# One-token attention and MLP on one core: row-form MLP products, a compact residual, w1 and w2 loaded behind the query weights, whole last K/V blocks

## The chip, the cores and the metric

The kernel runs on one core of a Trainium2 chip. The metric is device time in microseconds (us), from the start to the end of one execution; the number for a kernel is the median of its runs. The engines are PE (matrix products), DVE (vector), ACT (scalar), POOL (GpSimd) and SP, which here only issues transfers. Each engine runs its own instructions in order and waits on semaphores. SBUF is on-chip memory with 128 partitions, PSUM holds the results of PE in eight banks, and 16 DMA engines move data from HBM.

## The reference

```python
xn = _layernorm(x)
# attention: 32 query heads, 4 K/V heads, 65536 keys of 128, bf16
q = xn @ wq
p = softmax(q @ k^T * 128**-0.5); o = p @ v
A = o.reshape(1, 1, 4096) @ wo
# MLP branch on xn, S = 1
h  = gelu(layernorm(xn) @ w1)          # 1024 -> 1024
hs = concatenate([g0, g1, g2, g3]) @ w2
x1 = xn + hs
B  = x1 + gelu(layernorm(x1) @ w3) @ w4   # 1024 -> 3584 -> 1024
return x + A + B
```

g0 to g3 are the four quarters of h shifted along the sequence; with a sequence of one token each of them is zero, so the kernel multiplies w2 with a zero vector `g_bf`. K and V together are 134.2 MB; wq and wo are 8.4 MB each, w1 and w2 2.1 each, w3 and w4 7.3 each. The output is 1024 numbers in bf16.

## The kernel before

**Queues.** The kernel is written as five lists of operations (`_Q`), one an engine, in program order. `_op` and `_grp` append an operation or a group to a list and put the needed semaphore waits ahead of it, worked out from objects `_B` that remember the last write and the reads of a buffer. All large loads are issued by SP, in the order of the program, into one hardware queue.

**Attention.** The keys of a K/V head are cut into 8 tiles of 8192 keys, 32 tiles in all (`NT`). K and V come in blocks of two tiles, 4.19 MB each, 16 blocks of either (`issue_k(m)`, `issue_v(m)`, line 279), into two slots of `Kn` and `Vn`. Only the last block of K and of V (m = 15) is loaded as two halves (line 288), so that tile 30 needs only the first. I call these blocks K0 to K15 and V0 to V15. For tile n:
- `Ttr` (line 470): four DVE transposes of 128x1024 bring a tile of K into `X`;
- `QK` (480): 16 products of 512 columns into `S_ps`, on four column groups of PE at once;
- `stats1`, `MB`, `stats2`: the maximum over a row on DVE, spread over the partitions by a small product;
- `EXP` (508): the exponential on ACT; `PTr`: a product that orders the probabilities, and a DVE transpose `pT_f`;
- `PV` (531): 16 products with `Vn` into `OT_ps`; `FLASH` (541): ACT copies the result, POOL scales and adds it into `O_acc`.

The transposes of tile n+1 stand among tile n's DVE work: the first of them directly ahead of tile n's maximum (`Ttr(n + 1, [0])`, then `stats1(n)`), the others behind `EXP` and `PTr`. At the end of tile n the request for K block n/2+2 (even n) or V block (n-1)/2+2 (odd n) goes to SP's list; it waits until the slot is free, that is, until both tiles of the old block are transposed (K) or multiplied (V).

**Combine.** After the 8 tiles of a head, `combine_1` (553) sums and inverts the denominators and builds `cb_W`; `combine_2` (561) forms the head's normalized output with four f32 products (line 564) and three small DVE steps, giving `o_bf`. The combine of heads 0 to 2 stands inside the first tile of the next head; that of head 3 at the end.

**Weights.** The query weights are loaded first into slot 1 of `Kn` and `Vn`. A 14336-column buffer `W` holds w1, then w2, the halves of w3, wo of heads 0 and 1 in turn: each is loaded after one tile (0, 4, 8, 12, 16, 20) and multiplied after another (3, 7, 11, 15, 19, 23). w1, w2 and w3 are multiplied in column form (`mm_cols`, 362): the weight is the stationary operand, 128x128 at a time, and one column streams, so the result lies along the partitions. `out_resid` (409) adds the residual `acc` to the output with 32 small f32 products against an identity.

**Output.** `OUT_ps` collects 1024 outputs as rows of 256 on four partitions. `out_rows` (400, products at line 404) multiplies a stationary column of `o_bf` or `gh_bf` with rows of wo or w4, four products of 256 columns a row. Each group waits for the group before it, since all write `OUT_ps`.

**The end.** After tile 29 wo of heads 2 and 3 is requested; after tile 30, when K's slots are free, w4 in parts of 14, 8, 4 and 2 rows. PE's order behind tile 31 is: wo of head 2, combine of head 3, wo of head 3, w4 part by part. Then DVE casts the 4x256 outputs (line 631) and SP stores them.

## Time and profile before

| | |
|---|---|
| median of 3 runs | 402.89 us (402.86 to 402.99) |
| profiled execution, its span | 401.7 us; no time of its own is given for it beside the span, the median lies 1.2 us above |
| busy: DVE, PE, POOL, ACT | 228.4, 186.4, 61.8, 48.9 us |
| read from HBM | 169.87 MB, 423 GB/s over the span |
| mean granted PE clock | 0.586 |
| DVE waits for K | 67.4 us in 11 waits, the longest 9.2 |

The profile is one execution. Its first part gives the busy time of each engine; a second one cuts the span into 40 slices of 10 us, one digit a slice (9 is 90% busy or more), with the clock that PE was granted and the traffic. The table of DMA queues gives packets, megabytes and the share of the 16 engines' time. In the timeline a line has the start, the busy time, the engine, the line of the kernel, the operation, what it writes and reads, and in brackets the idle time before it and what ended that. Weight loads of PE (PEld) run beside the products.

### The profile page before, as it was taken

The page shows a single profiled execution, that of the slowest core. Times are in us where ns is not written, and L with a number is a line of the kernel's source. Part 1 is how long each engine was busy: PE and PEld are TensorE (multiplying, and loading weights), DVE is VectorE, ACT ScalarE, POOL GpSimd, SP SyncE. Part 2 cuts the span into 40 slices and gives each one's busy share as a digit, 9 for nine tenths or more (in the row PEclk, how much of TensorE's full clock was granted, in tenths as well). Part 3 has the DMA queues.
Part 4 walks back from the last instruction along what each step waited for, and adds up shares of the span by engine and source line. Part 5 has one row for each costly group of instructions (what it writes and reads, how often), then busy time and mean ns, then how long its engine had stood idle before and what let it go on. Part 6 is the DMA issues. An engine that isn't in the chain of part 4 may idle for free.

```text
span 401.7 us, 4776 instructions
## 1 busy us (share of the span) xinstructions
PE 186.4 (46%) x1859; PEld 78.5 (20%) x1875; DVE 228.4 (57%) x401; ACT 48.9 (12%) x128; POOL 61.8 (15%) x90
## 2 busy tenths in 40 slices
PE   0332325064525745285531965353433654444664
PEld 0211101021103511062110731121111311111132
DVE  0247566277816578255744287576836775788410
ACT  1000111011101011011110011111201111112100
POOL 5000003012211011110310101111110112112110
PEclk9985556556565556555655555656555656565566
DMA  8999999999999999999999999999999999999994
GB/s 359 424 418 438 445 418 424 460 419 421 436 447 419 429 435 435 422 436 445 420 428 450 426 419 441 441 419 428 434 439 421 447 432 424 426 425 436 437 416 207
DMA packets 7087, 170.19 MB, mean 424 GB/s; under 512 B 916, under 2 KB 920, under 8 KB 1048
## 3 DMA queue, kind: packets, MB, share of 16 engines
q1 hardware_dynamic: 6920, 169.87, 98.4%
q8 instruction: 15, 0.25, 0.2%
q14 instruction: 8, 0.07, 0.0%
q10 hardware_dynamic: 144, 0.00, 0.0%
HBM read 169.87 MB, written 0.00 MB: 423 GB/s over the span
## 4 chain that ended last, share of the span: by engine, by line
DMA 55%; DVE 24%; PE 16%; issue 2%; ACT 1%; SPq 0%; another core or an unknown queue 0%; POOL 0%; ACTq 0%
DMA Kn<-in_A_k_cache_dram 44%; DVE X L476 13%; DMA Kn<-in_B_w_dram 6%; DMA Vn<-in_A_wq_dram 5%; PE H_ps L366 4%; PE S_ps L488 3%; DVE pT_f L529 3%; PE OT_ps L536 3%; DVE mrow L495 3%; PE M_ps L366 1%; ACT p_sb L518 1%; PE PT_ps L527 1%; PE M_ps L564 1%; PE OUT_ps L404 1%; DVE Yall L393 1%
## 5 line engine op out<-in xcount | busy, mean ns | idle before, releaser
L476 DVE STREAM_TRANSPOSE X<-Kn 128x1024 f32<-128x1024 f32 x128 | 151.7, 1215 | 67.4 <-DMA Kn<-in_A_k_cache_dram 67.4
L536 PE MATMUL OT_ps<-Vn,pT_f 128*32 128x512 bf16 x512 | 60.7, 627 | 52.4 <-DVE pT_f L529 52.4
L488 PE MATMUL S_ps<-X,Yall 128*32 128x512 bf16 x512 | 59.1, 608 | 16.1 <-DVE X L476 16.1
L501 PE MATMUL MB_ps<-Rm,Lmat 128*128 128x16 bf16 x32 | 6.1, 192 | 90.1 <-DVE Rm L496 90.1
L550 POOL TENSOR_TENSOR O_acc<-O_acc,tmpO 128x513 f32<-128x513 f32 x28 | 32.8, 1172 | 88.6 <-ACT tmpO L544 88.6
L518 ACT ACTIVATE p_sb<-S_ps,brun 128x512 bf16<-128x512 f32 x32 | 22.0, 687 | 192.7 <-DVE brun L516 157.3
L548 POOL TENSOR_SCALAR O_acc<-O_acc,ff 128x513 f32<-128x513 f32 x28 | 19.5, 698 | 153.4 <-ACT ff L523 153.4
L495 DVE TENSOR_REDUCE mrow<-S_ps 128x1 f32<-128x512 f32 x32 | 21.6, 674 | 25.5 <-PE S_ps L488 25.5
L544 ACT ACTIVATE tmpO<-OT_ps 128x512 f32<-128x512 f32 x32 | 19.1, 598 | 108.0 <-PE OT_ps L536 108.0
L488 PEld LDWEIGHTS S_ps<-X,Yall 128*32 128x32 bf16 x512 | 16.6, 126 | 54.7 <-DVE X L476 38.2
L529 DVE STREAM_TRANSPOSE pT_f<-PT_ps 128x512 f32<-128x512 f32 x32 | 22.9, 716 | 6.1 <-PE PT_ps L527 4.2
L536 PEld LDWEIGHTS OT_ps<-Vn,pT_f 128*32 128x32 bf16 x512 | 14.6, 129 | 59.2 <-DVE pT_f L529 42.0
L501 PEld LDWEIGHTS MB_ps<-Rm,Lmat 128*128 128x128 bf16 x32 | 3.3, 102 | 114.9 <-DVE Rm L496 114.9
L527 PE MATMUL PT_ps<-p_sb,permR 128*128 128x512 bf16 x16 | 9.3, 580 | 21.4 <-ACT p_sb L518 21.4
L366 PEld LDWEIGHTS H_ps<-xn_bf,W 128*128 128x128 bf16 x224 | 14.4, 169 | 1.7 <-issue 1.7
L366 PE MATMUL H_ps<-xn_bf,W 128*128 128x1 bf16 x224 | 14.5, 202 | 0.0
L527 PEld LDWEIGHTS PT_ps<-p_sb,permR 128*128 128x128 bf16 x32 | 3.4, 105 | 41.4 <-ACT p_sb L518 41.4
L505 DVE TENSOR_REDUCE Bst<-MB_ps 128x1 f32<-128x16 f32 x32 | 5.6, 174 | 8.3 <-PE MB_ps L501 8.3
L330 PE MATMUL M_ps<-ln_s,ones_f 128*128 128x1 f32 x6 | 1.8, 362 | 17.3 <-DVE ln_s L329 17.3
L546 POOL COPY O_acc<-tmpO 128x513 f32<-128x513 f32 x4 | 2.4, 612 | 47.4 <-ACT tmpO L544 47.4
L404 PE MATMUL OUT_ps<-Kn,gh_bf 128*1 128x256 bf16 x112 | 5.6, 364 | 5.0 <-DMA Kn<-in_B_w_dram 5.0
L631 DVE CAST orow<-OUT_ps 128x256 bf16<-128x256 f32 x1 | 0.4, 425 | 12.7 <-PE OUT_ps L404 12.7
(109 smaller groups left out, 116.6 us busy)
## 6 DMA issues: line engine op xcount, KB each, us to landing
Kn<-in_A_k_cache_dram SPq DMA_DIRECT2D x15, 4096.0 KB, 27.3
Vn<-in_A_v_cache_dram SPq DMA_DIRECT2D x15, 4096.0 KB, 23.3
W<-in_B_w_dram SPq DMA_DIRECT2D x2, 3584.0 KB, 24.9
W<-in_A_wo_dram SPq DMA_DIRECT2D x3, 2048.0 KB, 23.8
Kn<-in_A_wq_dram SPq DMA_DIRECT2D x1, 4096.0 KB, 12.1
Vn<-in_A_wq_dram SPq DMA_DIRECT2D x1, 4096.0 KB, 21.2
W<-in_B_w_dram SPq DMA_DIRECT2D x2, 2048.0 KB, 33.8
Kn<-in_A_k_cache_dram SPq DMA_DIRECT2D x2, 2048.0 KB, 25.3
```

Source lines behind the costliest of these rows:

```text
L366: fns.append(lambda e, j=j, cx=cx: e.matmul(ps_tile[:, c0 + cx:c0 + cx + 1], lhs_fn(j - j0, cx), rhs_fn(j), start=(j == 0 and cx == 0), st ...
L404: fns.append(lambda e, lhs=lhs, rhs=rhs, jj=jj: e.matmul(OUT_ps[32 * jj:32 * jj + 1, 0:256], lhs, rhs[:, 256 * jj:256 * jj + 256], start=F ...
L476: _op(q_dve, lambda e, ix=ix: e.transpose(out=X32[:, xs, 1024 * ix:1024 * (ix + 1)], in_=Kn32[:, s, 4096 * half + 1024 * ix:4096 * half + ...
L488: fns.append(lambda e, we=we, cm=cm, mv=mv: e.matmul(S_ps[32 * cm:32 * cm + 32, :], Yall[:, h, we, :, :].rearrange("p a g -> p (a g)"), mv ...
L495: _op(q_dve, lambda e: e.reduce_max(mrow[:, m:m + 1], S_ps[:, :], axis=AX.X), reads=[b_S], writes=[b_mrow[m]])
L518: _op(q_act, lambda e: e.activation(p_sb[:, m, :], S_ps[:, :], ACTF.Exp, bias=brun[:, kn:kn + 1], scale=SCALE, accum_out=tmpO[:, m, 512:513]),
L527: _op(q_pe, lambda e: e.matmul(PT_ps[:, :], permR[:, :], p_sb[:, m, :], start=True, stop=True), reads=[b_p[m], b_const], writes=[b_PT])
L529: _op(q_dve, lambda e: e.transpose(out=pT_f[:, :], in_=PT_ps[:, :]), reads=[b_PT], writes=[b_pT])
L536: fns.append(lambda e, q=q, q4=q4: e.matmul(OT_ps[32 * q4:32 * q4 + 32, :], pT_bf[:, q, :, 1], Vn[:, s, 8192 * half + 512 * q:8192 * half ...
L544: _op(q_act, lambda e: e.activation(tmpO[:, m, 0:512], OT_ps[:, :], ACTF.Copy), reads=[b_OT], writes=[b_tmpO[m]], partial=True)
L548: _op(q_pool, lambda e: e.tensor_scalar(out=O_acc[:, :], in0=O_acc[:, :], scalar1=ff[:, m:m + 1], scalar2=0.0, op0=ALU.mult, op1=ALU.add), ...
L550: _op(q_pool, lambda e: e.tensor_tensor(out=O_acc[:, :], in0=O_acc[:, :], in1=tmpO[:, m, :], op=ALU.add), reads=[b_tmpO[m]], writes=[b_Oacc])
```

## The change

1. `mm_rows` takes the place of `mm_cols` for w1, w2 and w3: now the vector is the stationary operand, spread over 32 columns, and the weights stream, 256 or 448 columns at a time on four column groups. The result lies in rows; `to_cols` turns it into columns (ACT copy out of PSUM, an f32 product with a selecting matrix, a masked DVE multiplication, a DVE sum). New constants for it: `selQ`, `selS`, `mask32`.
2. `out_resid` builds a masked 128x256 tile on DVE and needs four f32 products.
3. w1 and w2 are requested directly behind the query weights, ahead of K0 and V0, w2 into slot 1 of `X`; their whole chain (`w12_pe`) runs before tile 0, the first half of w3 is requested behind V1 and multiplied after tile 7, the second half requested after tile 8 and multiplied after tile 15; wo of head 0 requested after tile 16 and multiplied after tile 23.
4. The last K and V blocks are loaded whole.
5. `O_acc` is double; the combines of heads 0 and 1 move to the ends of tiles 15 and 23, that of head 2 to the end of the kernel. `cb_W` now lies in `pT_f`.
6. wo of head 3 is requested after tile 24, w4's first 16 rows after tile 28, wo of heads 1 and 2 after tile 29 into slot 0 of `Vn`, w4's other 6, 4 and 2 rows after tile 30. The order on PE behind tile 31 is in the diff.
7. Some operations count on semaphores of their own, and waits of an engine on its own semaphore are left out where a reader's wait covers them.

The diff, cut to its core:

```diff
@@ _deps
         for s, v in b.w.items():
-            q.wait((s, v))
+            if s is not q.sem or not b.r:
+                q.wait((s, v))
@@ start
         load_rows(Vn[:, 1, :], b_V[1], "wqb", A_wq, 4, 4)
+        load_rows(W[:, 0:8192], [b_W], "w", B_w1, 0, 8)
+        load_rows(X[:, 1, :], b_X[1], "w2", B_w2, 0, 8)
@@ issue_kv
-            if m < NPAIR - 1:
-                _dma(q_sp, chan("%s%d" % (ch, s)), lambda e: e.dma_start(out=t[:, s, :], in_=src), writes=b_t[s])
-            else:
-                for hf in range(2):
-                    _dma(q_sp, chan("%sh%d" % (ch, hf)), lambda e, hf=hf: e.dma_start(out=t[:, s, 8192 * hf:8192 * hf + 8192], in_=src[:, 8192 * hf:8192 * hf + 8192]),
-                         writes=[b_t[s][hf]])
+            _dma(q_sp, chan("%s%d" % (ch, s)), lambda e: e.dma_start(out=t[:, s, :], in_=src), writes=b_t[s])
@@ MLP
+        def mm_rows(outs, lhs_fn, rhs_fn, j0, nj, njt, reads):
             fns = []
+            for j in range(j0, j0 + nj):
+                for sg, (tile, jj, c0, ln, _) in enumerate(outs):
+                    fns.append(lambda e, j=j, sg=sg, tile=tile, jj=jj, c0=c0, ln=ln: e.matmul(
+                        tile[32 * jj:32 * jj + 32, c0:c0 + ln], lhs_fn(j).broadcast_to([P, 32]), rhs_fn(j, sg),
+                        start=(j == 0), stop=(j == njt - 1), tile_position=(0, 32 * jj), skip_group_check=True))
...
+        def to_cols(parts, ln, n_in, mask, dst, b_dst, more):
...
+            for a, (tile, c0, bt, _, _) in enumerate(parts):
+                _op(q_act, lambda e, a=a, tile=tile, c0=c0: e.activation(hsb[:, a, :], tile[:, c0:c0 + ln], ACTF.Copy),
+                    reads=[bt], writes=[b_Wt] + more, partial=(a > 0))
+            _grp(q_pe, [lambda e, a=a, sl=sl, p0=p0: e.matmul(M0_ps[p0:p0 + sl.shape[1], 0:ln], sl, hsb[:, a, :], start=True, stop=True)
+                        for a, (_, _, _, sl, p0) in enumerate(parts)], reads=[b_Wt, b_const], writes=[b_M0])
...
@@ out_resid
+            _grp(q_pe, [lambda e, jj=jj: e.matmul(OUT_ps[32 * jj:32 * jj + 1, 0:256], maskA[:, jj, 0:1], A4, start=True, stop=False,
+                                                  tile_position=(0, 32 * jj), skip_group_check=True) for jj in range(4)],
+                 reads=[b_Wt, b_const], writes=[b_OUT], partial=True)
@@ loop and end
-        w4_parts = [(0, 14, 0, 0), (14, 8, 1, 0), (22, 4, 1, 8), (26, 2, 0, 14)]
+        w4_parts = [(0, 16, 0, 0), (16, 6, 1, 0), (22, 4, 1, 6), (26, 2, 1, 10)]
+        w12_pe()
+        w3_dma(0)
         Ttr(0, range(4))
         for n in range(NT):
...
-            if nb == 0 and h > 0:
-                combine_1(h - 1)
...
-            if nb == 0 and h > 0:
-                combine_2(h - 1)
...
+            if n == 7:
+                w3_pe(0)
+            elif n == 15:
+                combine_1(0)
+                w3_pe(1)
+                combine_2(0)
+            elif n == 23:
+                combine_1(1)
+                wo_pe(0)
+                combine_2(1)
...
+            if n == NT - 4:
+                w4_free(0)
+            elif n == NT - 3:
+                wo_dma(1)
+                wo_dma(2)
+            elif n == NT - 2:
+                for i in range(1, len(w4_parts)):
+                    w4_free(i)
-        wo_pe(HKV - 2)
-        combine_1(HKV - 1)
-        combine_2(HKV - 1)
-        wo_pe(HKV - 1)
-        for i in range(len(w4_parts)):
+        combine_1(2)
+        combine_2(2)
+        combine_1(3)
+        w4_pe(0)
+        combine_2(3)
+        wo_pe(3)
+        wo_pe(1)
+        wo_pe(2)
+        for i in range(1, len(w4_parts)):
             w4_pe(i)
```

## The prediction

> **What bounds the kernel now.** I read the page first: the slices, then the table of DMA queues.

> ```profile
> span 401.7 us, 4776 instructions
> ...
> DMA  8999999999999999999999999999999999999994
> ...
> q1 hardware_dynamic: 6920, 169.87, 98.4%
> q8 instruction: 15, 0.25, 0.2%
> ```

> One queue moves 169.87 MB and keeps the 16 DMA engines 98.4% busy. No compute engine is above 57%. Only the first and last slices are below 9. So the time is start, plus bytes over rate, plus what follows the last byte; a compute edit costs nothing until the queue runs dry or the work after the last loads overruns them. Next I read the timeline of DVE and PE around the last K blocks.

> ```profile
> 342.57 1.25 DVE L476 STREAM_TRANSPOSE X<-Kn 128x1024 f32<-128x1024 f32 x1 [4.64 <-DMA Kn<-in_A_k_cache_dram]
> ...
> 355.59 3.46 DVE L476 STREAM_TRANSPOSE X<-Kn 128x1024 f32<-128x1024 f32 x3
> ```

> The first line is block K14 landing (tile 28). The three transposes of the second line are the last two of tile 29 and, without a pause, the first of tile 30: the first half of K15 was there. K12 ended the same wait at 303.72, so four blocks (V12, K13, V13, K14) of 4.19 MB take 38.85 us: 9.71 us a block, 432 GB/s. Last I read the timeline of the end.

> ```profile
> 379.73 1.90 PE L536 MATMUL OT_ps<-Vn,pT_f 128*32 128x512 bf16 x16 [0.81 <-DVE pT_f L529]
> ...
> 381.41 1.73 PE L404 MATMUL OUT_ps<-Vn,o_bf 128*1 128x256 bf16 x32
> ...
> 383.50 0.38 PE L554 MATMUL M_ps<-O_acc,Dmat_f 128*128 128x1 f32 x2 [0.36 <-POOL O_acc L550]
> ...
> 384.67 1.16 PE L564 MATMUL M_ps<-O_acc,cb_W 128*128 128x128 f32 x8 [0.78 <-DVE cb_W L557]
> ...
> 386.92 1.88 PE L404 MATMUL OUT_ps<-W,o_bf 128*1 128x256 bf16 x32 [1.09 <-DVE o_bf L571]
> 390.37 2.98 PE L404 MATMUL OUT_ps<-Kn,gh_bf 128*1 128x256 bf16 x56 [1.58 <-DMA Kn<-in_B_w_dram]
> 395.21 1.04 PE L404 MATMUL OUT_ps<-Kn,gh_bf 128*1 128x256 bf16 x32 [1.85 <-DMA Kn<-in_B_w_dram]
> 397.63 1.02 PE L404 MATMUL OUT_ps<-Kn,gh_bf 128*1 128x256 bf16 x16 [1.38 <-DMA Kn<-in_B_w_dram]
> 398.85 0.59 PE L404 MATMUL OUT_ps<-Kn,gh_bf 128*1 128x256 bf16 x8 [0.19 <-DMA Kn<-in_B_w_dram]
> ```

> The last PV product ends at 381.63, and from 390.37 on PE waits for w4. PE finished wo at 388.80, 1.57 us early: that is the whole reserve in front of w4. After the last load only 0.59 us of PE, 0.42 of DVE and the store remain. The fourth view is the busy time in stretches of 3.41 us, the step in which the granted clock changes (the last columns are the clock, DMA share and GB/s).

> ```profile
> 379.40:382.81 3.41, 3.08 (x44) 1.52 (x48) 0.27 (x1) 0.60 (x1) 0.45 (x1) 0.50 1.01 428
> 382.81:386.22 3.41, 1.87 (x22) 1.28 (x14) 0.98 (x4) 0.00 (x0) 0.64 (x1) 1.00 1.02 434
> 386.22:389.64 3.42, 1.88 (x32) 0.97 (x32) 0.52 (x2) 0.00 (x0) 0.00 (x0) 0.50 0.94 402
> ```

> Full clock comes for one stretch behind a stretch with PE busy 3.08 of 3.41, and goes again. So 32 output-row products cost 1.88 us at half clock (386.92) and 1.04 at full (395.21).

> **The change part by part.** The sum is made against the profiled span of 401.7 us, in which the last product ends at 399.44; the median of 402.89 is 1.2 us above it, and I add differences to the median.

> *Loads.* The bytes are the same. The two last blocks lose two issues on SP (0.33 to 0.43 us each), hidden while more than one block is queued. Fewer PE instructions: w1, w2 and w3 go from 64, 64 and 224 one-column products to 32, 32 and 64 rows, the residual from 64 records to 8, and three row-to-column steps add about 8. That is 272 of 1859 products, and as many weight loads. If the 15 instruction packets shrink in proportion, two go. By the queue table one holds a DMA engine 0.2% x 16 x 401.7 / 15 = 0.86 us. The slowest engine gains between 0 and 1.7; I take 0.3, near nothing, because each packet falls on one engine of 16.

> *Start.* w1 and w2 (4.19 MB) now go in front of K0 and V0, which land 9.7 us later. The whole w1/w2 chain runs before tile 0. It begins when the second layer norm ends, 33.4: two row products of 32 (1.88 each), two ACT copies (at most 0.60), two f32 products over 256 columns (half of 2.07, the four of line 564 at 138.84), two pairs of DVE passes over 256 columns (0.42 each, as the output cast), the gelu (six steps, 1.3), two adds (0.4), the residual (0.43 DVE, 1.03 PE) and a layer norm (29.77 to 33.37: 3.6). Sum 15.6, so the first transpose moves from 33.3 to 49.0. Queued behind it on DVE are all of tile 0's transposes, and behind those the request for K2 on SP, which moves from 46.17 to about 62. But the queue then holds V0, K1, V1 and the first half of w3, until about 80: the query weights land at 22.5 (the chain's first load, 1.25 + 21.25), w1 and w2 at 32.2, then four blocks at 9.71 and 3.67 MB of w3 (8.5). Cover 18 us; cost 0. The two new constants on POOL (0.2 + 0.4 each at 0.93 to 5.06) are made before x lands at 13.05; cost 0.

> *Middle.* The w3 step at tile 15 was 7.2 us of PE and 1.4 of gelu. Now it is about 3.3 for a half of w3 (32 products of 448 columns at 0.104), then two copies (1.2), two f32 products over 448 columns (3.6), two DVE passes (1.4) and the gelu, with the first head's combine among them. DVE waits for K 67.4 us in 11 waits, up to 9.2 long, and a K request lands 27.3 us after issue against 9.7 of transfer: 17 us of cover. Cost 0. Fewer semaphore waits inside a tile: DVE's gaps there are 0.03 us; between 0 and 0.2 over the last two tiles, I take 0.1. SP's order at the end is new: w4's 16 rows after tile 28, two wo loads after tile 29, the rest of w4 once tile 31 is transposed, near 377; K15, V15, w4's 16 rows and the two wo loads fill the queue until 391. Cover 14; cost 0.

> *Last blocks whole.* K15 lands as one at 342.57 + 2 x 9.71 = 361.99. Tile 30's first transpose stands on DVE ahead of tile 29's maximum, so tile 29's statistics wait. From K14's wait to the next product of queries and keys took 349.89 - 342.57 = 7.32. So tile 30's moves from 365.53 to 369.31: 3.78 late, nothing catches up, and the last PV ends at 385.4. The DMA engines are 98.4% busy, yet the split is what let tile 30 start at about 358. [...]

> *The end.* After the last PV come, in order on PE: combine 2 (before, inside tile 24), combine 3's first product, w4's 16 rows, combine 3's second step, three wo groups (before: two), w4's 6, 4 and 2 rows. Each group of output rows waits for the one before it, which the 1.88 contains (pace 0.0537 + 0.16). At half clock:
> - 0.59 (line 554 at 136.72) + 0.79 (reciprocal, cb_W: 383.88 to 384.67) + 2.07 + 0.39 + 0.59 = 4.43 for combine 2 and the start of 3;
> - w4's 64 products 3.44; combine 3's second step 2.07 and 1.09 of DVE;
> - wo 3 x 1.88 = 5.64; w4's rest 1.45 + 1.02 + 0.59 = 3.06.

> Sum 19.7, so it ends at 405.1 against 399.44: +5.7. With full clock on every piece (0.38, 0.79, 1.16, 0.39, 0.38, 1.76, 1.16, 1.09, 3.12, 0.82, 0.60, 0.38) it is 12.0, ends at 397.4, earlier than w4's last rows at 398.8, and costs nothing. Between these ends I take one full-clock stretch wholly on PE work, which saves 3.4, as the rows show single stretches: +2.3. Less 0.3 and 0.1: **+1.9, 404.8 us**. [...]

> **Rivals.**
> - *The tail stays hidden* (other side). If full clock comes by about 392 and holds for two stretches, it saves up to 6.8, more than the 5.7, and w4's last landing decides again: 402.6. It decides from 5.3 us of full-clock work on. For it: w4's 64 products and the f32 step stand back to back for 5.5 us. Against it: 386.22, where full clock was lost behind the combine.
> - *Half clock to the end.* If the combine's f32 products don't bring full clock and w4's 64 straddle two stretches, 402.9 + 5.7 - 0.4 = 408.2. For it: from 386.22 to 393.05 the clock was half.
> - *Fewer fetches decide.* Tail hidden, and the slowest DMA engine loses both packets: 402.9 - 1.7 = 401.2. Against: it needs both on one engine.
> - *The start starves the queue.* Each us by which the w1/w2 chain passes its 18 us of cover costs one; if its 15.6 doubled, still nothing.

> **How the numbers follow.** About one full stretch on PE work: 0.55 (from one and a third, 5.7 - 4.5 - 0.4 = 0.8 over the median, 403.7, to a half, 5.7 - 1.7 - 0.4, 406.5). Half clock throughout: 0.15 (406.5 to 408.5). Tail hidden: 0.20 (402.2 to 403.6). Fetches: 0.07. Start starves or other: 0.03. A change under 0.2% (0.8 us) is about what cannot be told from none. Slower: 0.55 + 0.15 + 0.03, less 0.02 at the edge = 0.71; same 0.21; faster 0.08. The range leaves out the fetch case, and half clock's upper part: 402.3 to 407.5.

> **What would show it.** The first transpose of tile 30 ends a wait for K near 362; the last PV ends near 385; behind it PE has no wait for w4's last rows, or only a short one, and the last product ends after 400 with DMA idle before it. If DMA shows 9 in every slice, the queue never starved. Wrong would be: a PE wait for w4's last rows as before (clock), K15's wait absent, or a slice in the first quarter below 9.

## The result and the profile after

The changed kernel takes 406.38 us (median of 5 runs, 406.1 to 406.64) against 402.89 before (402.86 to 403.14): a ratio of 1.0084, 95% interval 1.0072 to 1.0096. It is 3.5 us slower. The prediction was 404.8, between 402.3 and 407.5.

The page of the changed kernel first: the span, the slices, and two rows of the DMA queues.

```profile
span 405.0 us, 4270 instructions
...
DMA  8999999999999999999999999999999999999991
...
q1 hardware_dynamic: 6632, 169.87, 97.5%
q8 instruction: 12, 0.20, 0.2%
```

The bytes are those of before, and every slice but the first and the last is at 9 again. The last one fell from 4 to 1: no transfer was late in the middle, and the added time is at the end, with the DMA engines idle.

The timeline of DVE around the last two K blocks:

```profile
343.12 1.25 DVE L509 STREAM_TRANSPOSE X<-Kn 128x1024 f32<-128x1024 f32 x1 [9.56 <-DMA Kn<-in_A_k_cache_dram]
...
356.10 2.33 DVE L509 STREAM_TRANSPOSE X<-Kn 128x1024 f32<-128x1024 f32 x2
362.45 1.25 DVE L509 STREAM_TRANSPOSE X<-Kn 128x1024 f32<-128x1024 f32 x1 [4.02 <-DMA Kn<-in_A_k_cache_dram]
```

K14 ends a wait at 343.12 (342.57 before). At 356.10 there are now two transposes, tile 29's last; before there were three, with the first of tile 30 behind them. That one now waits 4.02 us for the whole of K15, until 362.45.

The timeline of the end, with PE's products and, between them, DVE's scaling that builds `cb_W` (it writes `pT_f` now) and POOL's addition:

```profile
383.43 1.90 PE L575 MATMUL OT_ps<-Vn,pT_f 128*32 128x512 bf16 x16 [0.81 <-DVE pT_f L568]
...
386.09 1.57 DVE L598 TENSOR_SCALAR pT_f<-maskT,cb_rL 128x512 f32<-128x512 f32 x1
386.11 1.27 POOL L591 TENSOR_TENSOR O_acc<-O_acc,tmpO 128x513 f32<-128x513 f32 x1 [3.27 <-ACT tmpO L583]
...
387.72 2.07 PE L605 MATMUL M_ps<-O_acc,pT_f 128*128 128x128 f32 x8 [1.87 <-DVE pT_f L598]
...
390.75 3.58 PE L412 MATMUL OUT_ps<-Kn,gh_bf 128*1 128x256 bf16 x64
...
394.26 1.69 PE L605 MATMUL M_ps<-O_acc,pT_f 128*128 128x128 f32 x8
...
397.00 1.04 PE L412 MATMUL OUT_ps<-W,o_bf 128*1 128x256 bf16 x32 [1.05 <-issue]
...
399.42 1.04 PE L412 MATMUL OUT_ps<-Vn,o_bf 128*1 128x256 bf16 x32 [0.16 <-PE OUT_ps L412]
...
400.63 0.82 PE L412 MATMUL OUT_ps<-Kn,gh_bf 128*1 128x256 bf16 x24 [0.16 <-PE OUT_ps L412]
...
402.39 0.39 PE L412 MATMUL OUT_ps<-Kn,gh_bf 128*1 128x256 bf16 x8 [0.16 <-PE OUT_ps L412]
```

The last product ends at 402.78, where it ended at 399.44 before: 3.34 later, nearly all of the change in span (405.0 against 401.7). From 383.43 on PE waits for no transfer. The fourth view has the stretches in which the clock changes; after the busy times of PE, PEld, DVE, ACT and POOL come the granted clock, the DMA share and GB/s.

```profile
388.58:391.99 3.41, 2.93 (x34) 2.18 (x37) 1.50 (x5) 0.00 (x0) 0.00 (x0) 0.50 0.97 413
391.99:395.40 3.41, 3.41 (x49) 2.33 (x42) 0.00 (x0) 0.00 (x0) 0.00 (x0) 0.50 0.97 410
395.40:398.82 3.42, 2.20 (x61) 1.62 (x64) 0.84 (x3) 0.00 (x0) 0.00 (x0) 1.00 0.32 133
398.82:402.23 3.41, 2.91 (x88) 1.65 (x80) 0.00 (x0) 0.00 (x0) 0.00 (x0) 1.00 0.02 5
```

In the stretch from 395.40 the DMA share is 0.32, and after 398.82 it is 0.02: the last traffic of the loads is at 398.4, as in the kernel before, where the products of w4's last rows then began at 398.85. Here products run on until 402.78, 3.9 us past that. In this chain full clock comes only at 395.40 and then holds.

### The profile page after: what moved, and what is told of

Its sections match the earlier page's. It is cut to its first block, busy times and chain, and to the rows that moved or that the text cites. A ratio compares the mean times of both kernels' runs of the same rounds, so it can differ in the third digit from the quotient of the medians.

```text
span 405.0 us, 4270 instructions
## 1 busy us (share of the span) xinstructions
PE 178.6 (44%) x1587; PEld 61.3 (15%) x1603; DVE 236.7 (58%) x407; ACT 50.7 (13%) x132; POOL 64.0 (16%) x94
## 3 DMA queue, kind: packets, MB, share of 16 engines
q1 hardware_dynamic: 6632, 169.87, 97.5%
HBM read 169.87 MB, written 0.00 MB: 419 GB/s over the span
## 4 chain that ended last, share of the span: by engine, by line
DMA 50%; DVE 23%; PE 17%; issue 6%; ACT 2%; another core or an unknown queue 1%; POOL 0%; SPq 0%; ACTq 0%; DVEq 0%
DMA Kn<-in_A_k_cache_dram 44%; DVE X L509 13%; DMA Vn<-in_A_wq_dram 5%; PE S_ps L525 4%; DVE mrow L533 3%; PE OUT_ps L412 3%; PE OT_ps L575 2%; ACT p_sb L557 2%; PE M_ps L605 1%; PE PT_ps L566 1%; PE H_ps L430 1%; PE MB_ps L539 1%; PE M_ps L445 1%; DVE pT_f L568 1%; DVE Bst L545 1%
## 5 line engine op out<-in xcount | busy, mean ns | idle before, releaser
L525 PE MATMUL S_ps<-X,Yall 128*32 128x512 bf16 x512 | 57.7, 595 | 15.8 <-DVE X L509 15.8
L591 POOL TENSOR_TENSOR O_acc<-O_acc,tmpO 128x513 f32<-128x513 f32 x28 | 34.4, 1227 | 90.3 <-ACT tmpO L583 90.3
L557 ACT ACTIVATE p_sb<-S_ps,brun 128x512 bf16<-128x512 f32 x32 | 22.0, 688 | 185.3 <-DVE brun L555 153.0
L525 PEld LDWEIGHTS S_ps<-X,Yall 128*32 128x32 bf16 x512 | 14.3, 124 | 58.6 <-DVE X L509 41.3
L605 PE MATMUL M_ps<-O_acc,pT_f 128*128 128x128 f32 x32 | 7.0, 386 | 2.7 <-DVE pT_f L598 1.9
L357 POOL TENSOR_TENSOR ln_s<-ln_s,neghalf 128x1 f32<-128x1 f32 x3 | 1.7, 558 | 39.6 <-DVE ln_s L355 39.6
L430 PE MATMUL H_ps<-W,xn_bf 128*32 128x256 bf16 (+1 forms) x64 | 6.4, 482 | 1.4 <-DVE xn_bf L361 1.4
```

The lines of the kernel that those rows point to most:

```text
L525: fns.append(lambda e, we=we, cm=cm, mv=mv: e.matmul(S_ps[32 * cm:32 * cm + 32, :], Yall[:, h, we, :, :].rearrange("p a g -> p (a g)"), mv ...
L557: _op(q_act, lambda e: e.activation(p_sb[:, m, :], S_ps[:, :], ACTF.Exp, bias=brun[:, kn:kn + 1], scale=SCALE, accum_out=tmpO[:, m, 512:513]),
L591: _op(q_pool, lambda e: e.tensor_tensor(out=oa, in0=oa, in1=tmpO[:, m, :], op=ALU.add), reads=[b_tmpO[m]], writes=[b_oa])
```

## The experiments

The theory: two edits meet at the end. The whole K15 makes the last PV product 3.7 us later (385.33 against 381.63), and the new order puts more work behind it (head 2's combine, a third wo group, w4's 16 rows between the two steps of head 3's combine). PE's half clock makes that work long enough to pass the landing of w4. The main rival: the cost is in the rest of the change, that is in the start, the row form or the semaphores. Ratios are against runs of the kernel before on the same chip, with their 95% intervals.

**The last blocks in halves again.**

```diff
 # the changed kernel, issue_kv
-            _dma(q_sp, chan("%s%d" % (ch, s)), ..., writes=b_t[s])
+            if m < NPAIR - 1:
+                _dma(q_sp, chan("%s%d" % (ch, s)), ..., writes=b_t[s])
+            else:
+                for hf in range(2):
+                    _dma(q_sp, chan("%sh%d" % (ch, hf)), ..., writes=[b_t[s][hf]])
```

> The changed kernel, but K15 and V15 loaded as two halves again. Theory (the end decides: a late K15 and a longer chain of products behind the last PV): tile 30's first transpose no longer waits near 362, the last PV ends near 381.6 instead of 385.3, and the chain behind it, 17.4 us in the changed kernel's profile, ends near 399.1, about where w4's last rows land (398.9). Time 402.8 to 404.2, as the clock falls. Rival (the start, the row form or the new semaphores cost the 3.5 us): 405.5 to 406.6.

Measured: 402.99 us (402.78 to 403.55), ratio 1.0 (0.999 to 1.0009). The whole 3.5 us is gone. K14's wait on DVE and PE's end in its profile:

```profile
343.76 1.25 DVE L514 STREAM_TRANSPOSE X<-Kn 128x1024 f32<-128x1024 f32 x1 [9.57 <-DMA Kn<-in_A_k_cache_dram]
...
380.94 1.90 PE L580 MATMUL OT_ps<-Vn,pT_f 128*32 128x512 bf16 x16 [0.81 <-DVE pT_f L573]
...
398.58 0.61 PE L417 MATMUL OUT_ps<-Kn,gh_bf 128*1 128x256 bf16 x16 [0.16 <-PE OUT_ps L417]
399.56 0.39 PE L417 MATMUL OUT_ps<-Kn,gh_bf 128*1 128x256 bf16 x8 [0.38 <-DMA Kn<-in_B_w_dram]
```

The profile is that of the slowest of the ten runs (403.55). The last PV ends at 382.84, 2.5 us earlier than in the changed kernel and not the 3.7 expected: K14 ended its wait at 343.76 here, 1.19 later than in the kernel before, and the last PV is 1.21 later than there. The wait for K15 is gone. The chain behind the last PV is much the same, and it just reaches the landing: the last product waits 0.38 for its transfer, the group before it only for the group ahead. So in this run the reserve is some tenths of a microsecond.

**The merge alone, in the kernel before.**

```diff
 # the kernel before, issue_kv
-            if m < NPAIR - 1:
-                _dma(q_sp, chan("%s%d" % (ch, s)), ..., writes=b_t[s])
-            else:
-                for hf in range(2):
-                    _dma(q_sp, chan("%sh%d" % (ch, hf)), ..., writes=[b_t[s][hf]])
+            _dma(q_sp, chan("%s%d" % (ch, s)), ..., writes=b_t[s])
```

> The kernel before, with nothing changed but K15 and V15 loaded whole. Theory: tile 30 and the last PV come 3.8 us later (near 385.4), but in the old order little stands behind the last PV, so w4's last landing still decides: 402.8 to 403.5. Rival (the merge alone makes the loss): 406.0 to 406.7.

Measured: 402.67 us (402.58 to 402.96), ratio 0.9994 (0.9984 to 1.0003): no loss. PE's end:

```profile
383.17 1.90 PE L531 MATMUL OT_ps<-Vn,pT_f 128*32 128x512 bf16 x16 [0.81 <-DVE pT_f L524]
...
386.95 0.58 PE L549 MATMUL M_ps<-O_acc,Dmat_f 128*128 128x1 f32 x2 [0.17 <-POOL O_acc L545]
...
397.52 0.61 PE L399 MATMUL OUT_ps<-Kn,gh_bf 128*1 128x256 bf16 x16 [0.57 <-DMA Kn<-in_B_w_dram]
398.73 0.39 PE L399 MATMUL OUT_ps<-Kn,gh_bf 128*1 128x256 bf16 x8 [0.61 <-DMA Kn<-in_B_w_dram]
```

The last PV ends at 385.07, as late as in the changed kernel (385.33). But head 3's combine starts at 386.95, not at 390.27, and wo and w4's first rows end in time: PE waits 0.57 and 0.61 for the last two parts. So the late block costs nothing by itself; it uses up most of the reserve that the first profile showed. That reserve is PE's four waits for w4 there, 1.58, 1.85, 1.38 and 0.19, together 5.0 us. Where the transfer is already there, a group of output rows still waits 0.16 for the group ahead (393.52 in this run), so some 4.4 us of it could be used. The merge took 3.44 and left 0.86, the 0.57 and 0.61 less 0.16 each.

**Head 2's combine out of the end.**

```diff
 # the changed kernel
+            if n == 24:
+                combine_1(2)
+                combine_2(2)
...
-        combine_1(2)
-        combine_2(2)
         combine_1(3)
```

> The changed kernel with head 2's combine moved from the end to behind tile 24. Theory: the last PV still ends near 385.3; head 3's combine then starts when POOL has added the last tile, near 387.4, instead of 390.3, and everything behind comes 2.8 us earlier, ending between w4's landing and 400 at the same clock: 403.0 to 404.6. If the clock stays at half through the wo products, up to 405.5. Rival (head 2's combine is hidden): 406.1 to 406.6.

Measured: 403.46 us (402.98 to 403.93), ratio 1.0011 (1.0002 to 1.002): some 2.9 of the 3.5 us.

```profile
383.54 1.90 PE L575 MATMUL OT_ps<-Vn,pT_f 128*32 128x512 bf16 x16 [0.81 <-DVE pT_f L568]
387.55 0.59 PE L595 MATMUL M_ps<-O_acc,Dmat_f 128*128 128x1 f32 x2 [2.11 <-POOL O_acc L591]
...
400.09 0.39 PE L412 MATMUL OUT_ps<-Kn,gh_bf 128*1 128x256 bf16 x8 [0.16 <-PE OUT_ps L412]
```

With the PV as late as in the changed kernel, head 3's combine starts at 387.55, when POOL is done, and not at 390.27. In this profile, that of the slowest of the ten runs (403.93), the last product ends at 400.48 and still waits for nothing but the group before it: the chain decides by about 1 us.

**PE kept busy for the clock.**

```diff
 # the changed kernel
+        def fill(n, k):
+            if n >= NT - 2:
+                _grp(q_pe, [lambda e: e.matmul(H_ps[:, :], ident_bf[:, :], W[:, 0:512], start=True, stop=True)] * k, reads=[b_W, b_const], writes=[b_H])
...
             stats1(n)
+            fill(n, 2)
             MB(n)
...
             Ttr(n + 1, [1])
+            fill(n, 3)
             PTr(n)
             Ttr(n + 1, [2, 3])
+            fill(n, 1)
             PV(n)
```

> The changed kernel with idle products added on PE in tiles 30 and 31 (six of 512 columns a tile, into a bank that is free, results unused), so that PE is busy in nearly every stretch. Theory (the granted clock sizes the end): full clock from before the last PV to the end, the chain behind the last PV takes about 14 us instead of 17.4, and the time is 402.9 to 404.0. Rival (the end is made of waits and DVE steps, not of PE's clock): 406.0 to 407.0.

Measured: 402.93 us (402.7 to 404.33), ratio 1.0001 (0.9992 to 1.0011). Nothing is taken away, twelve products are added, and the kernel is 3.4 us faster. The stretches of this kernel:

```profile
377.70:381.10 3.40, 3.35 (x22) 0.61 (x10) 1.36 (x5) 0.48 (x1) 0.50 (x1) 0.50 0.94 395
381.10:384.50 3.40, 2.21 (x21) 0.74 (x20) 1.13 (x3) 0.99 (x4) 0.71 (x2) 0.99 1.05 448
...
391.30:394.80 3.50, 2.56 (x84) 1.55 (x72) 0.00 (x0) 0.00 (x0) 0.00 (x0) 1.00 0.99 418
```

Behind the stretch with PE busy 3.35 the clock is 0.99 to 1.00 up to the last loads. Its timeline:

```profile
382.65 1.05 PE L575 MATMUL OT_ps<-Vn,pT_f 128*32 128x512 bf16 x16 [0.59 <-DVE pT_f L568]
...
384.25 0.49 DVE L598 TENSOR_SCALAR pT_f<-maskT,cb_rL 128x512 f32<-128x512 f32 x1
384.49 1.38 POOL L591 TENSOR_TENSOR O_acc<-O_acc,tmpO 128x513 f32<-128x513 f32 x1 [2.21 <-ACT tmpO L583]
...
393.14 1.04 PE L412 MATMUL OUT_ps<-Vn,o_bf 128*1 128x256 bf16 x32 [0.16 <-PE OUT_ps L412]
...
395.18 0.83 PE L412 MATMUL OUT_ps<-Kn,gh_bf 128*1 128x256 bf16 x24 [0.99 <-DMA Kn<-in_B_w_dram]
```

The last PV ends at 383.70, the third wo group at 394.18; in the changed kernel it was 385.33 and 400.46. From PV to there it is 10.5 us instead of 15.1. Of these 4.6, 1.1 is not PE's products: `cb_W` took 0.49 here and 1.57 in the changed kernel; it began 0.24 before POOL's addition here, and 0.02 there. Then PE waits for w4 again (0.99). So half clock is the third condition of the loss, beside the late block and the long chain: with any one of the three taken away, at most 0.6 us of the 3.5 is left.

**Both undone.** The changed kernel with the two edits of the first and third experiment.

> The changed kernel with both undone: K15 and V15 in halves, head 2's combine behind tile 24. What is left of the change is the early w1 and w2, the row form, the compact residual, the semaphores and w4's 16 rows ahead of head 3's combine. Theory (only the end cost anything): PE waits for w4's last rows again, by over 1 us, and the time is that of the kernel before within 0.3 us: 402.6 to 403.2. Rival (a small part of the loss, 0.5 us or more, sits in the rest): 403.5 or more.

Measured: 403.03 us (402.72 to 403.19), ratio 1.0002 (0.9993 to 1.0012).

```profile
393.56 1.04 PE L417 MATMUL OUT_ps<-Vn,o_bf 128*1 128x256 bf16 x32 [0.16 <-PE OUT_ps L417]
395.52 0.83 PE L417 MATMUL OUT_ps<-Kn,gh_bf 128*1 128x256 bf16 x24 [0.92 <-DMA Kn<-in_B_w_dram]
397.95 0.61 PE L417 MATMUL OUT_ps<-Kn,gh_bf 128*1 128x256 bf16 x16 [1.61 <-DMA Kn<-in_B_w_dram]
399.20 0.39 PE L417 MATMUL OUT_ps<-Kn,gh_bf 128*1 128x256 bf16 x8 [0.64 <-DMA Kn<-in_B_w_dram]
```

PE waits 0.92, 1.61 and 0.64 for the last three parts; it waited for them before the change too (1.85, 1.38 and 0.19). What is left of the change, the start, the row form, the residual, the semaphores, is worth nothing that can be measured: the rival falls. That holds for a kernel whose end is hidden. The third wo group and w4's 16 rows ahead of head 3's second step are still in this run; no run takes them out singly.

**`cb_W` on ACT.**

```diff
 # the changed kernel, combine_1
-            _op(q_dve, lambda e: e.tensor_scalar(out=cb_W[...], in0=maskT[...], scalar1=cb_rL[:, 0:1], scalar2=None, op0=ALU.mult),
+            _op(q_act, lambda e: e.activation(cb_W[...], maskT[...], ACTF.Copy, scale=cb_rL[:, 0:1]),
```

> The changed kernel with the scaling that builds cb_W (0.49 us alone, 1.58 at the end beside POOL's addition) moved from DVE to ACT. Theory (DVE's step waits for POOL): on ACT it takes some 0.6 us with POOL running, head 2's four products start near 386.8 instead of 387.7, and the time falls by 0.9 to 405.3 to 405.8, unless the clock steps fall elsewhere (404.5 to 406.2). Rival (the step is slow because of where it writes): it stays at 1.4 us or more, and the time at 406.1 to 406.6.

Measured: 405.19 us (404.46 to 405.71), ratio 1.0053 (1.0038 to 1.0068): 1.2 us less than the changed kernel.

```profile
386.19 0.72 ACT L598 ACTIVATE pT_f<-maskT,cb_rL 128x512 f32<-128x512 f32 x1
386.21 1.27 POOL L591 TENSOR_TENSOR O_acc<-O_acc,tmpO 128x513 f32<-128x513 f32 x1 [3.05 <-ACT tmpO L583]
...
386.96 2.08 PE L605 MATMUL M_ps<-O_acc,pT_f 128*128 128x128 f32 x8 [1.01 <-ACT pT_f L598]
```

Beside the same addition on POOL, ACT needs 0.72, and writes the same `pT_f`: the place is not the reason. Head 2's four products start at 386.96 instead of 387.72; from the last PV to them it is 1.53 us instead of 2.39, which is 0.86 of the 1.2. In this profile head 3's f32 products took 1.16 instead of 1.69, so the clock gave part of the rest.

**A smaller last load.** Both undone, and w4's parts end with one row and one row instead of two.

> The run with both undone, and w4's last part cut to one row (four products, 0.26 MB) instead of two. Theory (what stands behind the last landing is paid in full): 0.1 to 0.2 us less behind the last landing, 402.7 to 402.9, hardly to be told from the run with both undone. Rival (a transfer more has a cost of its own): 403.1 or more.

Measured: 402.93 us (402.55 to 403.27), ratio 0.9998 (0.9989 to 1.0007): nothing that can be told from 403.03.

```profile
398.81 0.38 PE L417 MATMUL OUT_ps<-Kn,gh_bf 128*1 128x256 bf16 x4 [0.15 <-PE OUT_ps L417]
399.36 0.38 PE L417 MATMUL OUT_ps<-Kn,gh_bf 128*1 128x256 bf16 x4 [0.16 <-PE OUT_ps L417]
```

The last row's products wait 0.16 for the group before them, not for the transfer. Here the split only traded the landing for that wait.

**Without w1 and w2.** Both undone, and 4.19 MB less:

```diff
 # the changed kernel, both undone
-        load_rows(W[:, 0:8192], [b_W], "w", B_w1, 0, 8)
-        load_rows(X[:, 1, :], b_X[1], "w2", B_w2, 0, 8)
...
         def w12_pe():
-            mm_rows(...); to_cols(...); gelu(...); mm_rows(...); to_cols(...)
-            _op(q_dve, lambda e: e.tensor_tensor(out=x1[:], in0=xn[:], in1=hs[:], op=ALU.add), ...)
-            _op(q_dve, lambda e: e.tensor_tensor(out=acc[:], in0=acc[:], in1=hs[:], op=ALU.add), ...)
+            _op(q_dve, lambda e: e.tensor_copy(x1[:], xn[:]), reads=[b_xn], writes=[b_x1])
             out_resid()
             layer_norm(x1, b_x1, xn3, xn3_bf, b_xn3, 208)
```

> The run with both undone, without w1 and w2: since the sequence has one token, their result meets the output only as a product with a zero vector, so both loads (4.19 MB), both products and the gelu between are left out and x1 is xn. Theory (with the end hidden, bytes over rate are the time): 9.7 us less than the run with both undone, 393.1 to 393.6. Rival (the end or the tiles take over as the bound before all of it is gained): 394 to 398.

Measured: 393.34 us (393.12 to 393.42), ratio 0.9759 (0.9746 to 0.9772), faster than both kernels.

```profile
span 391.9 us, 4116 instructions
...
DMA  8999999999999999999999999999999999999994
```

```profile
385.42 0.83 PE L415 MATMUL OUT_ps<-Kn,gh_bf 128*1 128x256 bf16 x24 [1.55 <-DMA Kn<-in_B_w_dram]
...
389.09 0.60 PE L415 MATMUL OUT_ps<-Kn,gh_bf 128*1 128x256 bf16 x8 [0.36 <-DMA Kn<-in_B_w_dram]
```

The second view is PE's end: it waits for w4 as before. 403.03 - 393.34 = 9.69 us for 4.19 MB, the 9.71 of a block. With the end hidden, bytes over rate are the time.

## Why the prediction was right, and where it was short

- *What bounds.* Right. The traffic of the loads ends at 398.4 in both kernels, and taking bytes away takes 9.7 us a block away.
- *Loads.* The gain of 0.3 from fewer instruction packets did not come. The packets fell from 15 to 12, one more than I worked out, and the loads still end at the same time. Why isn't settled: the profile doesn't show on which DMA engine a packet falls.
- *Start.* Right. The first transpose starts at 48.63 (49.0 by the sum), K2 is requested at 61.43 (62), and every slice stays at 9. The run with both undone has this start and loses nothing.
- *Middle.* Right: no slice below 9. The 0.1 from fewer semaphore waits can't be seen in the total.
- *Last blocks whole.* The step was right: the wait ends at 362.45 (361.99), tile 30's products start at 369.72 (369.31), the last PV ends at 385.33 (385.4). What the text did not say is that this edit costs nothing in the old order, as the second experiment shows. In the new order, splitting the block again brought the 3.4 us back, with the DMA engines 97.5% busy in the changed kernel.
- *The end.* The mechanism was right; the term was too small. The chain from PV to the last product took 17.45 us; the prediction had 19.7 at half clock less 3.4, that is 16.3. Two terms and the clock were mis-sized. `cb_W` took 1.57 instead of 0.49, 1.08 more. Each group of output rows waits 0.16 for the one before it, in five places, which I had thought to be inside the 1.88: 0.8 more. Against that, full clock saved about 4.2 instead of 3.4: on the wo groups 3 x 0.84, on w4's last parts 1.24, on head 3's second step 0.45. 1.08 + 0.8 - 0.8 = 1.1, and 0.4 of gains that did not come, is 1.5 of the 1.6 us by which the forecast was low. That it came so near is in part luck: the 1.9 us that were missing and the 0.8 of clock partly cancel.
- *The reserve.* The reading was wrong, though the sum did not use it. The text calls the 1.57 us in front of w4's first part the whole reserve; all four waits count, some 4.4 us. With it the loss adds up: the last PV 3.70 later, and the chain behind it 17.45 us against 13.45 before without those 4.4 of waits, 4.00 longer. 3.70 + 4.00 - 4.36 = 3.34, by which the last product ends later.
- *The clock.* "One full-clock stretch" came as one long grant at the end, from 395.40. The stretch in which w4's 64 products began also held the combine's gap: PE was busy 2.93 of 3.41 in it, and the stretch behind it stayed at 0.50. That one had PE busy 3.41 of 3.41, and 1.00 followed; behind the fourth experiment's 3.35 of 3.40 it was 0.99. So full clock came some 3.4 us later than the 392 that the first rival needed, and with that 402.6 was out of reach. But the rows give no threshold in PE's busy time: in the kernel before, 2.68 (from 389.64) was followed by 1.00, and 3.42 and 3.41 (from 222.38, one-column products of w3) were followed by 0.50. What a stretch must hold stays open.
- *Rivals.* "The tail stays hidden" was the close one: it needed savings of 5.3 us from full clock, 7.2 with the two terms that I missed, and the kernel got 4.2. The fourth experiment is that rival made true. "Half clock to the end", the fetches and the starved start fell.

## What to carry to other kernels

When one queue of loads sets the time, find the reserve in front of its last landing (all of PE's waits for the last loads, here some 4.4 us) and charge every edit that moves work behind the last dependent block against it, together: two edits that are each free (402.67 with the merge alone, 402.99 with the new order alone) can pass it as a pair (406.38). Price such a chain with the slow clock (here 0.50, at which 32 output-row products took 1.88 us, and 1.04 at 1.00), with the wait between groups (0.16), and with what other engines do at that moment (`cb_W` took 1.57 beside POOL's addition, 0.49 alone). And with all else hidden, fewer bytes were what helped here: 4.19 MB whose product is with zeros were worth 9.7 us, and no order of the work came below 402.67.
